# Sums, gates and weight preparations of a retention and two-FFN kernel, redistributed over the engines and stages of one core

## The chip, the core and the metric

The kernel runs on one core of one Trainium2 chip. TensorE (PE) multiplies matrices from SBUF into PSUM, VectorE (DVE), ScalarE (ACT) and GpSimd (POOL) work elementwise, and SyncE (SP) mostly issues DMA transfers; each engine executes its own instructions in the order in which they stand. The metric is the device time in microseconds of one launch. Before the change it is 1136.62 us, the median of 2 runs (1136.56 to 1136.67).

## The reference

A retention (linear attention with decay) feeds two feed-forward layers without residuals. Everything is float32; 3072 tokens, model width 512, inner width 2048:

```python
for t in range(S):                      # B, H, S, D = 4, 8, 768, 64
    state = gamma * state + k[:, :, t] (outer) v[:, :, t]
    y[:, :, t] = (1 / sqrt(D)) * q[:, :, t] @ state
x = y as (B * S, H * D)
h = x @ moe_w_in;   x = maximum(0.01 * h, h) @ moe_w_out          # leaky ReLU
h = x @ moe2_w_in;  x = (h / (1 + exp(-1.702 * h))) @ moe2_w_out  # gated by a sigmoid
```

The weights arrive as 64-bit floats, so the kernel itself turns each pair of 32-bit words into a float32.

## The kernel before

Every product is made of three matmuls on split operands: each float32 operand becomes a rounded high part (a cast on ACT) and a low part (a subtraction on DVE), and high*low, high*high and low*high are summed in PSUM. On top of that, each FFN product is done by a Strassen-Winograd scheme with 7 products instead of 8, whose operands and weights are sums and differences of quarter blocks. The program runs through six stages, and I give each a letter:

- **A, retention**, 24 steps, with the raw words of the first input weights loaded, converted and split beside it. The first tiles of FFN 1's input layer follow each step.
- **B**: 16 plain products `ffn_in(m, x1, ...)` of 12 matmuls with 256 columns, on the token columns left over. Each is emptied by ACT with a leaky ReLU, and stored with a DMA that ACT issues.
- **C, `First` of FFN 1** (`first1`): 24 pairs of (token block, q), 7 products of 6 matmuls with 384 columns each. `tick()` follows each product and runs whatever was put off by a number of ticks (`Later.at`), then `beside1`, which gives out at most one step of a weight preparation per tick.
- **D, `Second` of FFN 1** (`second1`): 168 items (3 blocks, 7 forms, 8 values of q), 6 matmuls of 512 columns per item. For each item ACT casts the operand (`high`, four items ahead), and DVE subtracts (`low`, three ahead); I call the latter a low. 96 operands' sums (`total`, four forms times 8 times 3) make the forms' operands from the loaded blocks; of these, the ones of form 5 are on DVE and the other 72 on POOL (`nc.gpsimd` given to `second1`).
- **E, `First` of FFN 2** (`first2`): 32 pairs, as C, with the sigmoid gate.
- **F, `Second` of FFN 2** (`second2`): as D, with all 96 sums on DVE, then a transpose and the store of the result.

A weight preparation (`Prep`) makes one half of a row of weights for a later stage: two loads of 256 KB of raw words, two ACT functions (`words_scalar`), four DVE operations (`words_vector`, lines 182 to 188), a rounding addition (`round_up`, line 197), three subtractions that form the Strassen sums (`total`, by way of line 157), and a store of 448 KB. There are 48, 16 each for `1o` (FFN 1 out), `2i` (FFN 2 in) and `2o`. Before, the first 20 (`N_P`) are done beside B and C, the next 15 (`N_S`) in D by the smaller form `Packed`, the last 13 in E; rounding and sums are on POOL in all three. SP's queue is in order too: a store of a sum that isn't there yet holds up the loads behind it.

The gate of E (`inner`, `gate`) is a Sigmoid on ACT into an extra tile, and a product on DVE with the value itself (line 615). The result then goes into `gd2` by a DMA that ACT issues.

Of the kernel before, what the change touches and what calls it, by code (L numbers as in the profile page):

```python
# [21 lines left out]
P = 128  # L22
# [10 lines left out]
T1 = 384  # L33
# [25 lines left out]
N_P, N_S = 20, 15  # L59
# [31 lines left out]
def retention_two_ffn(ctx: ExitStack, tc: tile.TileContext, qkv, consts, small, w1i, w1o, w2i, w2o, scratch, out):  # L91
# [167 lines left out]
    def retention():  # L259
# [129 lines left out]
        for s in range(len(steps)):  # L389
# [28 lines left out]
    class Prep:  # L418
# [36 lines left out]
        def steps(self):  # L455
# [4 lines left out]
            out = [lambda: None, lambda: words_scalar(self.f, self.low, raw[:, :, 1])]  # L460
            out += [lambda step=step: step(self.f, raw[:, :, 1]) for step in words_vector]
            return out

        def finish(self, clock, others, e=nc.gpsimd, wait=5):
            round_up(self.f, self.low, e)
            self.total(e)
            clock.at(wait, self.store)
            if others:
                others.pop(0).load()

    class Packed(Prep):
# [7 lines left out]
        def sums(self, e=nc.gpsimd):  # L479
# [48 lines left out]
    class First:  # L528


        def __init__(self, at, clock, src, dst, first, n, gated, weight, p_banks):
# [3 lines left out]
            self.g, self.s, self.p = (ring(at[k], T1) for k in ("g", "s", "p"))  # L535
# [37 lines left out]
        def run(self, done, step, beside):  # L573
# [19 lines left out]
            def inner(n, r, f, src=None, made=None):  # L593
# [15 lines left out]
                def gate(src, t):  # L609
                    s = next(self.s)[:, :w]  # L610
                    nc.scalar.activation(out=s, in_=src, func=AF.Sigmoid, scale=1.702)  # L611

                    def product():
                        dst = tile() if t is None else t
                        nc.vector.tensor_tensor(out=dst, in0=src, in1=s, op=ALU.mult)
                        later.at(2, lambda: store(dst))

                    later.at(1, product)

                if made is not None:  # L620
                    t = tile()
                    made(t)
                    if self.gated:
                        later.at(1, lambda: gate(t, t))
                        return
                    src, dst = t, t
                    later.at(1, lambda: nc.scalar.activation(out=dst, in_=src, func=AF.Lrelu))
                    later.at(3, lambda: store(dst))
                elif self.gated:
                    gate(src, None)  # L630
                else:
                    dst = tile()
                    nc.scalar.activation(out=dst, in_=src, func=AF.Lrelu)
                    later.at(2, lambda: store(dst))
# [596 lines left out]
```

## Time and profile before

| what | value |
|---|---|
| median of the runs | 1136.62 us |
| the profiled execution, its own time | 1130.26 us |
| its span, first to last instruction | 1128.5 us |
| PE busy | 1054.5 us, 93% of the span |
| DVE busy | 890.0 us, 79% |
| ACT busy | 616.8 us, 55% |
| POOL busy | 393.9 us, 35% |
| granted TensorE clock, mean | 0.978 |
| DMA | 241.63 MB, mean 214 GB/s |

How to read it: an engine's busy time covers the whole span, and a matmul's end is modelled, so a matmul that waits within its pipeline counts as busy. What bounds the kernel shows stage by stage, in the busy time of each engine within the stage, in the time that PE waits, and in the pace of PE. The granted clock is given in parts of full speed.

### The profile page before, as it was taken

What the parts mean: (1) busy time and instruction counts of PE and PEld (TensorE: products, weight loads), DVE (VectorE), ACT (ScalarE), POOL (GpSimd) and SP (SyncE); (2) the same over time, 40 slices, a digit from 0 to 9 for tenths busy, and PEclk for the clock granted to TensorE, in tenths of its full rate; (3) what the DMA queues carried; (4) which work ended last, traced back from release to release, by engine and by line L of the source; (5) the groups of instructions that cost most, each with busy time, mean ns of one, the idle gap of its engine ahead of it and who ended that gap; (6) DMA issues with size and microseconds to landing.
All of it is one profiled execution on the core that took longest, in us unless ns stands there. A gap on an engine that the chain in (4) does not pass through costs nothing.

```text
span 1128.5 us, 18170 instructions
## 1 busy us (share of the span) xinstructions
PE 1054.5 (93%) x6198; PEld 920.2 (82%) x6198; DVE 890.0 (79%) x1300; ACT 616.8 (55%) x1256; POOL 393.9 (35%) x353
## 2 busy tenths in 40 slices
PE   9999979999999869888888799999999999999998
PEld 6777878989998647656666499999999988888886
DVE  5998456886536999898889967768677899788786
ACT  5776355755666544443443476656566665544543
POOL 2332135675301684389349831343432000000000
PEclk9999989999999889998999999999999999999999
DMA  9999678889478454823744466564849852843723
GB/s 341 361 382 399 222 246 274 282 271 322 167 265 277 137 175 150 266 85 113 248 165 135 162 225 230 178 234 175 296 148 329 272 176 72 196 139 84 215 75 75
DMA packets 185420, 241.63 MB, mean 214 GB/s; under 512 B 59248, under 2 KB 134896, under 8 KB 182256
## 3 DMA queue, kind: packets, MB, share of 16 engines
q1 hardware_dynamic: 157376, 208.19, 55.5%
q10 hardware_dynamic: 27952, 32.29, 8.0%
q8 instruction: 48, 0.79, 0.3%
q14 instruction: 44, 0.36, 0.1%
HBM read 146.58 MB, written 93.85 MB: 213 GB/s over the span
## 4 chain that ended last, share of the span: by engine, by line
PE 56%; DVE 20%; DMA 11%; issue 5%; POOL 4%; ACT 2%; SPq 1%; ACTq 1%; DVEq 0%; POOLq 0%
PE psum L589 28%; PE psum L790 20%; DVE c L157 8%; PE psum L252 4%; DMA c<-w1o 2%; DVE h L157 2%; DMA h<-qkv 2%; POOL b L755 2%; DMA d<-gd 1%; DVE b L755 1%; DMA gd<-d 1%; PE psum L290 1%; DMA b<-gd 1%; PE psum L320 1%; DMA h<-wdt 1%
## 5 line engine op out<-in xcount | busy, mean ns | idle before, releaser
L790 PE MATMUL psum<-c,h 128*128 128x512 f32 x1008 | 258.6, 414 | 49.3 <-DVE c L157 45.9
L790 PEld LDWEIGHTS psum<-c,h 128*128 128x128 f32 x1008 | 195.7, 198 | 112.0 <-DVE c L157 66.8
L790 PE MATMUL psum<-e,h 128*128 128x512 f32 x768 | 179.3, 389 | 0.0
L790 PEld LDWEIGHTS psum<-e,h 128*128 128x128 f32 x768 | 144.1, 188 | 29.9
L742 ACT CAST c<-b 128x512 fp32r<-128x512 f32 x96 | 58.7, 621 | 97.9 <-PE psum L790 47.8
L589 PE MATMUL psum<-c,h 128*128 128x384 f32 x576 | 110.1, 334 | 0.3 <-DVE d L637 0.3
L589 PE MATMUL psum<-b,h 128*128 128x384 f32 x576 | 110.1, 334 | 0.2 <-ACT psum L673 0.2
L157 DVE TENSOR_TENSOR h<-h 128x256 fp32r<-128x256 f32 (+3 forms) x144 | 86.0, 636 | 30.1 <-ACT h L898 15.2
L157 DVE TENSOR_TENSOR c<-b,c 128x512 fp32r<-128x512 f32 x96 | 102.2, 1095 | 4.4 <-ACT c L742 3.8
L589 PEld LDWEIGHTS psum<-c,h 128*128 128x128 f32 x576 | 100.7, 188 | 0.6 <-DVE d L637 0.6
L589 PEld LDWEIGHTS psum<-b,h 128*128 128x128 f32 x576 | 100.7, 188 | 0.6 <-ACT psum L673 0.6
L611 ACT ACTIVATE d<-psum 128x384 f32<-128x384 f32 x96 | 47.1, 491 | 62.7 <-PE psum L589 56.2
L742 ACT CAST e<-a 128x512 fp32r<-128x512 f32 x77 | 47.7, 622 | 43.3 <-PE psum L790 21.9
L589 PE MATMUL psum<-f,h 128*128 128x384 f32 x336 | 67.5, 335 | 1.5 <-DVE b L637 1.5
L589 PE MATMUL psum<-d,h 128*128 128x384 f32 x288 | 59.2, 340 | 7.3 <-ACT psum L673 7.3
L755 POOL TENSOR_TENSOR d<-d,a 128x512 f32<-128x512 f32 x24 | 42.6, 1802 | 65.2 <-PE psum L790 65.2
L589 PEld LDWEIGHTS psum<-f,h 128*128 128x128 f32 x336 | 59.0, 188 | 2.0 <-DVE b L637 1.8
L637 DVE TENSOR_TENSOR psum<-psum,g 128x384 f32<-128x384 f32 x56 | 31.5, 563 | 36.6 <-PE psum L589 34.3
L157 DVE TENSOR_TENSOR e<-a,e 128x512 fp32r<-128x512 f32 x77 | 52.3, 685 | 8.3 <-ACT e L742 7.7
L589 PEld LDWEIGHTS psum<-d,h 128*128 128x128 f32 x288 | 51.1, 191 | 8.7 <-ACT psum L673 8.7
L589 PE MATMUL psum<-a,h 128*128 128x384 f32 x288 | 58.1, 337 | 0.1
L589 PE MATMUL psum<-e,h 128*128 128x384 f32 x288 | 57.5, 334 | 0.0
(186 smaller groups left out, 2064.1 us busy)
## 6 DMA issues: line engine op xcount, KB each, us to landing
gd<-d ACTq DMA_DIRECT2D x128, 192.0 KB, 3.8
h<-qkv SPq DMA_DIRECT2D x21, 1024.0 KB, 8.7
b<-gd SPq DMA_DIRECT2D x72, 256.0 KB, 4.5
d<-gd SPq DMA_DIRECT2D x72, 256.0 KB, 4.8
a<-gd SPq DMA_DIRECT2D x48, 256.0 KB, 5.2
c<-w1i SPq DMA_DIRECT2D x16, 512.0 KB, 7.7
c<-w1o SPq DMA_DIRECT2D x32, 256.0 KB, 4.8
e<-w2o SPq DMA_DIRECT2D x26, 256.0 KB, 4.2
```

The lines of the kernel that those rows point to most:

```text
L157: e.tensor_tensor(out=o, in0=x, in1=y, op=ALU.subtract)
L252: nc.tensor.matmul(out=h, lhsT=w[:, a, k], rhs=x[c][:, k], start=(i == 0), stop=(i == 3 * NP - 1), skip_group_check=True)
L290: nc.tensor.matmul(out=ps[:, e, n], lhsT=kT[r, n], rhs=qT[r, n], start=True, stop=True, skip_group_check=True)
L320: nc.tensor.matmul(out=out(n, e), lhsT=v[:, n, r], rhs=sm[:, e, n], start=(n < 2), stop=(c == 0), skip_group_check=True)
L589: nc.tensor.matmul(out=t, lhsT=w(k, a), rhs=x[:, b, k], start=(start and m == 0), stop=(m == 5), skip_group_check=True)
L611: nc.scalar.activation(out=s, in_=src, func=AF.Sigmoid, scale=1.702)
L637: nc.vector.tensor_tensor(out=o, in0=x, in1=y, op=ALU.add)
L742: nc.scalar.copy(out=t[:, 0], in_=self.block_of(*item))
L755: e.tensor_tensor(out=a(*s[0]), in0=a(*s[1]), in1=a(*s[2]), op=s[3])
L790: nc.tensor.matmul(out=t[:, j], lhsT=w[:, j, a], rhs=x[:, b], start=(new and q == 0 and m == 0), stop=(q == NQ - 1 and m == 2), skip_group ...
```

## The change

Six things change.

1. In D, the 72 operands' sums move from POOL to DVE (`total`); the argument that chose the engine is gone.
2. In all preparations, rounding and sums move from POOL to DVE. The six or seven steps of a preparation become four: the ACT pair, two DVE operations, two more, then rounding, sums, store (one tick later) and the next load.
3. The preparations are divided 26 / 6 / 16 over C, D and E, in place of 20 / 15 / 13. In D a `Packed` starts every 18 items from item 30, in place of every 9 from item 6.
4. E's gate is one ACT function, `Gelu_apprx_sigmoid`, straight into the tile that is stored. Sigmoid, product and the extra tiles fall away.
5. The raw words of the first three preparations are loaded in the last three steps of A, in place of the second tick of B.
6. Tiles and delays in C: the ring of six result tiles starts in another area, stores are issued 4 ticks after the ACT function instead of 2 (the last pairs: 2), preparations come every 4 or 5 ticks in B and 5 or 6 in C, and `second1` begins its loads one pair later, 2 ticks apart instead of 3.

The core of the diff:

```diff
-N_P, N_S = 20, 15
+N_P, N_S = 26, 6
...
+            if s >= len(steps) - 3:
+                todo[s - len(steps) + 3].load()
...
-            out = [lambda: None, lambda: words_scalar(self.f, self.low, raw[:, :, 1])]
-            out += [lambda step=step: step(self.f, raw[:, :, 1]) for step in words_vector]
-            return out
-
-        def finish(self, clock, others, e=nc.gpsimd, wait=5):
+            f, low, high, e = self.f, self.low, raw[:, :, 1], nc.vector
+            vector = lambda k: [step(f, high) for step in words_vector[k : k + 2]]
+            return [lambda: words_scalar(f, low, high), lambda: vector(0), lambda: vector(2), lambda: self.sums(e)]
+
+        def sums(self, e):
             round_up(self.f, self.low, e)
             self.total(e)
-            clock.at(wait, self.store)
-            if others:
-                others.pop(0).load()
+
+        def give(self, clock, behind, others):
+            def end():
+                clock.at(1, self.store)
+                if others:
+                    others.pop(0).load()
+
+            *steps, last = self.steps()
+            behind.extend(steps + [lambda: (last(), end())])
...
-        def sums(self, e=nc.gpsimd):
+        def sums(self, e=nc.vector):
...
-                def gate(src, t):
-                    s = next(self.s)[:, :w]
-                    nc.scalar.activation(out=s, in_=src, func=AF.Sigmoid, scale=1.702)
-
-                    def product():
-                        dst = tile() if t is None else t
-                        nc.vector.tensor_tensor(out=dst, in0=src, in1=s, op=ALU.mult)
-                        later.at(2, lambda: store(dst))
-
-                    later.at(1, product)
...
+                def gate(dst, src):
+                    if self.gated:
+                        nc.scalar.activation(out=dst, in_=src, func=AF.Gelu_apprx_sigmoid)
+                    else:
+                        nc.scalar.activation(out=dst, in_=src, func=AF.Lrelu)
+                    later.at(1 if self.gated else 4 if n + 2 < len(pairs) else 2, lambda: store(dst))
...
-                e = nc.vector if i == 5 else self.e
-                e.tensor_tensor(out=a(*s[0]), in0=a(*s[1]), in1=a(*s[2]), op=s[3])
+                nc.vector.tensor_tensor(out=a(*s[0]), in0=a(*s[1]), in1=a(*s[2]), op=s[3])
...
-    left = [5]
-
-    def beside1(free):
+    left, apart = [3], [4]
+
+    def beside(clock):
         left[0] -= 1
         if left[0] <= 0 and todo:
-            p = todo.pop(0)
-            left[0] = beside1.apart
-            behind.extend(p.steps()[1:] + [lambda: p.finish(later2, waiting, nc.gpsimd, 3)])
+            left[0] = apart[0] + len(todo) % 2
+            todo.pop(0).give(clock, behind, waiting)
...
-        if n >= 6 and n % 9 == 6 and packed:
+        if n >= 30 and (n - 30) % 18 == 0 and packed:
             packed.pop(0).start(later)
```

Three places of the program show how instructions move. The first is DVE in the first block of D. Here c is the ring of split operands (a low writes it), a, b and d are the loaded blocks, h the weights, e a result. Before:

```order
L157 TENSOR_TENSOR c_3324<-b,c_3324 128x512 x2
L157 TENSOR_TENSOR c_3324<-a,c_3324 128x512
L157 TENSOR_TENSOR c_3358<-a,c_3358 128x512 x2
L157 TENSOR_TENSOR c_3324<-a,c_3324 128x512 x2
L182 TENSOR_SCALAR f<-f 128x512
L184 TENSOR_SCALAR f<-f 128x512
L186 TENSOR_SCALAR f<-f 128x512
L188 SCALAR_TENSOR_TENSOR f<-f 128x512
L798 TENSOR_TENSOR e<-psum,e 128x1024
```

and now:

```order
L749 TENSOR_TENSOR d<-d,a 128x512
L157 TENSOR_TENSOR c_3466<-a,c_3466 128x512 x2
L749 TENSOR_TENSOR d<-d,a 128x512
L157 TENSOR_TENSOR c_3504<-a,c_3504 128x512
L749 TENSOR_TENSOR d<-d,a 128x512
L157 TENSOR_TENSOR h_418<-h_418 128x128 x2
L157 TENSOR_TENSOR c_3504<-a,c_3504 128x512
L157 TENSOR_TENSOR h_1548<-h_1548 128x128 x2
L157 TENSOR_TENSOR c_3466<-a,c_3466 128x512
L749 TENSOR_TENSOR d<-d,a 128x512
L157 TENSOR_TENSOR h_418<-h_418 128x128 x2
L792 TENSOR_TENSOR e<-psum,e 128x1024
```

The sums (line 749, before 755) now stand between the lows, and the four word operations of a preparation (lines 182 to 188) have left this stretch.

The second place is DVE in the early pairs of C: c and e are tiles of a preparation, h the factors' splits, and line 637 (now 632) is the addition in PSUM that a later product waits for. Before:

```order
L637 TENSOR_TENSOR psum<-psum,g 128x384
L182 TENSOR_SCALAR c_233<-c_233 128x512
L184 TENSOR_SCALAR c_1633<-c_1633 128x512
L186 TENSOR_SCALAR c_1633<-c_1633 128x512
L637 TENSOR_TENSOR a_490<-psum,g 128x384
L157 TENSOR_TENSOR h_418<-h_418 128x256
L157 TENSOR_TENSOR h_1542<-h_1542 128x512
L157 TENSOR_TENSOR h_418<-h_418 128x256
L188 SCALAR_TENSOR_TENSOR c_1633<-c_1633,c_233 128x512
```

and now:

```order
L182 TENSOR_SCALAR c_233<-c_233 128x512
L184 TENSOR_SCALAR e_80<-e_80 128x512
L186 TENSOR_SCALAR e_80<-e_80 128x512
L188 SCALAR_TENSOR_TENSOR e_80<-e_80,c_233 128x512
L197 ISA e_80<-c_233,e_80 128x1024
L157 TENSOR_TENSOR e_80<-e_80 128x256
L157 TENSOR_TENSOR e_80<-e_80 128x128 x2
L632 TENSOR_TENSOR b<-psum,g 128x384
```

Rounding (line 197) and the three subtractions of a preparation have come into DVE's queue, ahead of the addition that PE needs.

The third place is SP's queue at the end of A. xd takes the retention's results, the load of b brings C's first input back, the loads of h from wdt are the factors of C's weights, and the loads of c from w1o are raw words. Before:

```order
L215 DMA wdt<-e_80 128x1024
L167 DMA xd_3_68<-a 128x2x384
L169 DMA xd_3_68<-a 64x2x384 x2
L552 DMA b<-xd_1_66 128x3072
L894 DMA h_1542<-wdt 128x512
L894 DMA h_1542<-wdt 128x256
L894 DMA h_418<-wdt 128x256
L437 DMA c_233<-w1o 128x2x256 x6
```

and now:

```order
L215 DMA wdt<-e_80 128x1024
L439 DMA c_233<-w1o 128x2x256 x4
L167 DMA xd_3_68<-a 128x2x384
L169 DMA xd_3_68<-a 64x2x384 x2
L439 DMA c_233<-w1o 128x2x256 x2
L560 DMA b<-xd_1_66 128x3072
L894 DMA h_1548<-wdt 128x512
L894 DMA h_1548<-wdt 128x256
L894 DMA h_418<-wdt 128x256
```

Four of the six raw loads now stand ahead of A's last store, and two between it and the load of b.

## Rows read from the trace of the kernel before

**Rows 1.** Windows by stage, B to F: us, busy by engine, clock, DMA share, GB/s.
```profile
133.00:164.00 31.00, 25.65 (x209) 25.27 (x205) 12.55 (x16) 12.90 (x27) 9.45 (x7) 0.89 0.78 243
164.00:352.00 188.00, 178.70 (x1012) 176.17 (x1010) 119.26 (x179) 115.57 (x239) 82.89 (x86) 0.99 0.77 261
352.00:661.00 309.00, 260.13 (x1019) 197.68 (x1020) 279.96 (x307) 146.16 (x272) 197.94 (x149) 0.94 0.50 168
661.00:894.00 233.00, 232.47 (x1340) 231.83 (x1339) 173.03 (x313) 142.93 (x289) 67.70 (x69) 1.00 0.67 235
894.00:1128.50 234.50, 230.51 (x1020) 190.28 (x1018) 197.11 (x311) 116.85 (x200) 0.02 (x1) 1.00 0.51 137
```

**Rows 2.** Waits of PE over the span: us in total, times, longest.
```profile
PE psum L790 <- DVE c L157: 45.9, 24, 4.3
PE psum L589 <- ACT psum L673: 7.5, 5, 2.8
PE psum L252 <- ACT a L256: 5.4, 1, 5.4
```

**Rows 3.** Groups of DVE in D, two of its three lows: busy, mean ns.
```profile
L157 DVE TENSOR_TENSOR c<-b,c 128x512 fp32r<-128x512 f32 x92 | 99.5, 1113 | 4.4 <-ACT c L742 3.8
...
L157 DVE TENSOR_TENSOR c<-a,c 128x512 fp32r<-128x512 f32 x24 | 27.1, 1171 | 0.0
```

**Rows 4.** Groups of POOL in D, one of its three sums.
```profile
L755 POOL TENSOR_TENSOR d<-d,a 128x512 f32<-128x512 f32 x24 | 42.6, 1802 | 65.2 <-PE psum L790 65.2
```

**Rows 5.** Groups of DVE in F, where POOL is silent.
```profile
L755 DVE TENSOR_TENSOR a<-b,a 128x512 f32<-128x512 f32 x47 | 32.2, 685 | 5.3 <-DMA b<-gd 5.3
...
L798 DVE TENSOR_TENSOR c<-psum,c 128x1024 f32<-128x1024 f32 x9 | 11.0, 1217 | 0.0
```

**Rows 6.** Timeline of DVE early in D: start, us, what.
```profile
361.50 0.69 DVE L755 TENSOR_TENSOR b<-d,b 128x512 f32<-128x512 f32 x1
362.10 0.69 DVE L157 TENSOR_TENSOR c<-b,c 128x512 fp32r<-128x512 f32 x1
...
366.18 1.53 DVE L157 TENSOR_TENSOR h<-h 128x128 fp32r<-128x128 f32 x2
...
369.25 0.42 DVE L182 TENSOR_SCALAR f<-f 128x512 uint32<-128x512 uint32 x1
...
371.10 0.69 DVE L157 TENSOR_TENSOR c<-b,c 128x512 fp32r<-128x512 f32 x1
```

**Rows 7.** Timeline of POOL, the same place.
```profile
362.57 4.79 POOL L755 TENSOR_TENSOR d<-d,a 128x512 f32<-128x512 f32 x1 [65.21 <-PE psum L790]
```

**Rows 8.** Pace of PE: timeline in C, then a window within F.
```profile
339.84 1.20 PE L589 MATMUL psum<-f,h 128*128 128x384 f32 x6
340.88 1.20 PE L589 MATMUL psum<-a,h 128*128 128x384 f32 x6
...
931.00:959.00 28.00, 28.00 (x125) 23.20 (x124) 27.31 (x45) 15.17 (x28) 0.00 (x0) 1.00 0.26 72
```

**Rows 9.** Timeline of ACT in B, around the wait of PE.
```profile
149.01 1.23 ACT L898 CAST h<-h 128x256 fp32r<-128x256 f32 x3 [7.72 <-DMA h<-wdt]
...
151.85 0.67 ACT L178 ACTIVATE c<-c 128x512 f32<-128x512 f32 x1 [0.88 <-DMA c<-w1o]
```

**Rows 10.** Window at the end of A; timeline of SP's queue.
```profile
125.00:130.00 5.00, 5.00 (x73) 3.96 (x72) 2.25 (x3) 0.60 (x1) 0.00 (x0) 1.00 0.14 54
...
139.40 2.12 SPq L894 DMA_DIRECT2D h<-wdt  x3
```

**Rows 11.** Groups of ACT in E: the Sigmoid, the table load.
```profile
L611 ACT ACTIVATE d<-psum 128x384 f32<-128x384 f32 x96 | 47.1, 491 | 62.7 <-PE psum L589 56.2 <-DVE d L615 3.1 <-DVE d L637 1.7
...
L1032 ACT ACT_TABLE_LOAD x1 | 1.3, 1283 | 0.0
```

**Rows 12.** Groups of DVE in A: the rounding addition, where DVE does it.
```profile
L197 DVE CUSTOM_DVE_ANT_0 b<-c,b 128x1024 uint16<-128x1024 uint16 x9 | 6.1, 681 | 0.0
```

**Rows 13.** Waits of ACT, 125 to 350 us: one of several for C's result tiles.
```profile
ACT a L633 <- DMA gd<-a: 6.1, 3, 4.7
```

More of the change, by code (lines that the diff above doesn't have):

```diff
@@ L872, in rows @@
             return slice(n * T2, (n + 1) * T2)
+    c1 = Area("c1")
+    prep_rings = ring([(c2, 4), (c2, 8), (c2, 0)], 4, P, 2), ring(run_of(c1, 2, 4) + [(e4, 0)], 8, P)
+    names = [(kind, n) for kind in ("1o", "2i", "2o") for n in range(2 * NQ)]
+    todo = [Prep(*name, prep_rings) for name in names[:N_P]]
+    waiting, behind = todo[3:], collections.deque()
     retention()
@@ L953, in retention_two_ffn @@
         later2.tick()
[L954 removed]
+        beside(later2)
     def step1(n):
[L957 removed]
         if n == 0:
+            apart[0] = 5
             form(7, 0, 0, 1)
@@ L964, in step1 @@
             later2.at(9, factors[n + 3].low)
-        if n == 2 * NQ:
+        if n == 17:
             first1.g = ring(g_at[1], T1)
-        if n == 18:
-            assert not todo and not behind
-            second1.begin(later2, 0, NQ, 4, 24, 3)
+        if n == 19:
+            assert not todo
+            second1.begin(later2, 0, NQ, 4, 24, 2)
     def done_p(blk, q):
@@ L981, in done_p @@
             second1.loads(3 if q == NQ - 2 else 5)
-    first1.run(done_p, step1, beside1)
+    first1.run(done_p, step1, lambda free: beside(later2))
     while behind:
@@ L1031, in done1 @@
         if m == 51:
-            nc.scalar.activation(out=p_a.view(0, 4), in_=first2.raw[:, 0, :4], func=AF.Sigmoid, scale=1.702)
+            nc.scalar.activation(out=p_a.view(0, 4), in_=first2.raw[:, 0, :4], func=AF.Gelu_apprx_sigmoid)
         if m in (45, 47, 49):
@@ L1058, in retention_two_ffn @@
     todo = [Prep(*name, prep_rings2) for name in names[N_P + N_S :]]
-    behind, waiting = collections.deque(), []
+    behind, waiting, apart[0] = collections.deque(), [], 100
+    left[0] = 100
     def step2(n):
@@ L1067, in step2 @@
             todo[n - 4].load()
-        if n == 5:
+        if n == 6:
             waiting.extend(todo[2:])
-        if 6 <= n < 24 and n % NQ in range(1, 7) and todo:
-            p = todo.pop(0)
-            behind.extend([lambda: behind.extendleft(reversed(p.steps() + [lambda: p.finish(later2, waiting)]))])
+            left[0], apart[0] = 0, 7
         if n == 26:
@@ L1085, in done2 @@
         second2.loads(3 if q == NQ - 2 else 5)
-    def beside2(free):
-        if behind and free:
-            behind.popleft()()
-    first2.run(done2, step2, beside2)
+    first2.run(done2, step2, lambda free: beside(later2) if free or todo else None)
     while behind:
```

40 lines of the change are left out of this document (12 added, 28 removed).

## The prediction

> **What bounds the kernel now.** I read the windows by stage first, since one average over six stages with different limits says little. Then I read the waits of PE, the groups of DVE and POOL in the stage that loses most, and the timeline there, because means of contended work hide what an operation costs alone.
>
> The pace that PE can hold is the yardstick. In C a product of 6 matmuls starts 1.04 us after the one before; in F 125 matmuls of 512 columns fill 28 us, 0.224 us each [rows 8]. At that pace C needs 24 x 7 x 1.04 = 174.7 us and takes 188. D needs 168 x 6 x 0.224 = 225.8 us and takes **309**. E needs 32 x 7 x 1.04 = 233 us and takes 233, and F does the same matmuls as D in 234.5 with its tail [rows 1]. So E and F run at PE's pace, C loses 13 us, and D loses 83, more than all other stages.
>
> D's loss is DVE's lateness. [...] DVE is busy 280 of 309 us [rows 1], but a low in D takes 1113 to 1171 ns [rows 3], where the same shape takes 685 in F, with POOL silent [rows 5]. At 361.5 us, ahead of POOL's first sum, two such operations start 0.60 us apart [rows 6]. POOL's sum, begun at 362.57, lasts 4.79 us, while DVE goes on at its pace [rows 7], and then a pair of small DVE operations takes 1.53 us [rows 6]. So the two engines exclude each other where both read two SBUF operands: POOL's sums take 1.8 us on average [rows 4], and its 198 us in D [rows 1] are mostly paid for by DVE.
>
> **The change, part by part.**
>
> *D, sums and lows.* DVE gets the 72 sums (24 it has). There are 164 lows left in this stage and 96 sums, 260 operations. What does one cost when POOL is silent? Its duration is 0.69 us, but the next starts after 0.60 [rows 6], so I take 0.60: 156 us. To these come 11 evacuations of 1.2 us [rows 5], 13 us; 40 weight splits of 128 or 256 columns, some 12 us (pro rata from 0.60 for 512, an estimate); and 5 us of the next stage's forms. Preparations: six in place of 15. Four word operations take 371.10 - 369.25 = 1.85 us [rows 6], rounding 0.68 [rows 12], the three subtractions no more than 3 x 0.60, by their columns about 1.0. That is 3.5 us each, 21 for six. Sum: **207 us of DVE for 226 us of PE.**
>
> So PE becomes the bound of D. Locally it is closer: by the order, 38 of the 168 items have about 53 us of DVE work ahead of them (all the splits, a preparation, three forms' sums), and PE reaches that place after 51 us, with lows three items (4 us) ahead. Later blocks have less. I take 3 us of waiting: D falls from 309 to 229, **-80**. What is late next there would be ACT's casts, but ACT is busy 146 us now [rows 1] and loses nine preparations.
>
> [...] That such operations overlap is what the two starts in [rows 6] show, so the trace decides for 0.60; the durations remain as the dear end: 260 x 0.69 + 13 + 12 + 5 + 6 x 4.2 = 235 us, with 12.5 of lag at the worst place. D is then 243, -66. The cheap end is no wait at all, -83.
>
> *C, six more preparations, rounding and sums on DVE.* DVE receives 26 x (0.68 + 1.0) + 6 x 1.85 = 55 us. Its present 132 us in B and C [rows 1] shrink, as POOL keeps only the forms' sums there: with 0.09 us of overlap on some 200 operations and the contention gone, to 95 or 100. That makes 150 to 187 us of 219. As the preparations end by pair 18, the stretch in which they run is over nine tenths full, and the additions that PE waits for stand behind bursts of 1.3 us; PE goes on for three products, 3.1 us, before it needs one. I cost this at 3 us. Against that stand the 13 us that C loses now, of which 7.5 are waits for ACT's copies [rows 2], late behind raw words, forms and result tiles that land late [rows 13]. The loads now go out as soon as DVE has rounded, not after POOL's turn. The copies at C's start stay late, since B's ACT work grows by a preparation. I take half the loss as recovered, **-6**, from -13 (all) to +10 (DVE's durations, DMA as below).
>
> *First raw words in A.* B's wait of 5.4 us ends behind ACT [rows 2], and ACT's queue stood first 7.72 us for the factors from `wdt`, then 0.88 for raw words [rows 9]. The change takes away the latter, and puts the words' two functions (0.67 each) ahead of the wait: 2 us. The former stays. SP issues those loads at 139.4 [rows 10], and one of the three raw loads, 512 KB, now stands just before; at the 300 GB/s or so that such stretches move, it delays them by 1.7 us. The other two fall into a stretch with a DMA share of 0.14 [rows 10] and cost nothing. **-1**, between 0 and -7.
>
> *E, the gate.* DVE loses 128 products, and gets three more preparations and all sums. It was busy 173 of 233 us, and PE waits for neither engine there, so this gains nothing. ACT has the same 128 functions of 384 columns. The trace holds no Gelu; Sigmoid takes 491 ns [rows 11], and its cost lies between that and 0.67 us, the longest ACT function of [rows 9] (for 512 columns). ACT is busy 143 us of 233 [rows 1]: 128 x 0.18 more lies in that cover. Were the cover gone, it would cost 23 us. **0**, at most +6 where a block begins.
>
> *F and A*: nothing in them changes but A's loads. 0.
>
> Sum: -80 - 6 - 1 = -87. The profiled execution of 1130.26 us lies 6.4 below the median of 1136.62; its own would become 1043, and with the same distance the median **1050 us**.
>
> **The rivals.**
>
> *DVE stays the bound in D* (operations cost their durations, or words arrive late and hold its queue). For it: 94% DVE load at those prices, and a late start's lag isn't made good. Against it: F runs the same lows and sums with 197 us of DVE busy and no PE wait. -66 - 1 - 3: about 1066. Chance 0.18.
>
> *C is starved.* Six more preparations move 6 x 0.96 MB through a stage at a DMA share of 0.77 [rows 1], and result tiles are stored two ticks later in a ring of six, so that ACT, which already waits on this ring [rows 13], waits more. If C loses 10 more instead of 6 less: 1066 again, or 1080 with the first rival. Chance 0.12.
>
> *DVE's 1.1 us in D isn't POOL's doing* but that of PSUM, DMA or clock in this stage. Then the sums come on top, at the same rate: 280 us - 9 x 2.2 (words) + 72 x 1.1 + 6 x 3 = 357 us, 48 more than 309: 1136.6 + 48 - 7 = **1178**, slower. It decides at (309 - 51) / 260 = 0.99 us per operation. For it: only the means in [rows 3]. Against it: within the same stage, 0.60 us as long as POOL is held off [rows 6]. Chance 0.03.
>
> *The gate reloads tables.* If Gelu and the copies beside it didn't share a set, ACT would load a table (1283 ns, [rows 11]) at each change, some six per pair: 32 x 6 x 1.28 = 246 us on top of 143, 156 over E's 233: 1050 + 156 = 1206. The order has two table loads in the whole program, as before. Chance 0.01. [...]
>
> **How the numbers follow.** The forecast has 0.62; its own range is 1035 to 1062. The other 0.04 are things I haven't seen, half of them above 1080. With both dear ends (D -66, C +5) the time is 1075, with both cheap ones 1136.6 - 83 - 13 - 7 = 1033. The range is 1033 to 1076. Two per cent, 23 us either way, is about what a measurement tells from no change. Only the 1178 and 1206 cases and half of the unseen ones come out above 1113: faster 0.94, same 0.02, slower 0.04.
>
> **What would show it right or wrong.** Right: D's window about 229 us long with clock near 1.00, lows and sums near 0.69 us long and 0.60 apart, POOL nearly idle there until D's end, DVE's work in D about 207 us by starts (some 235 by durations). The wait on lows at most 5 us. C at 182, still with a wait at its start; B's wait on ACT still there, shorter. Wrong: lows above 0.9 us without POOL; waits of PE on line 632 in C of more than 8 us in total; DMA waits of ACT on C's tiles above 25; a Gelu above 0.67 us.

## The result, and the profile after

The changed kernel takes **1082.18 us**, the median of 2 runs (1082.13 to 1082.23), against 1136.62: a ratio of 0.952, 95% interval 0.948 to 0.956. Four further runs of it (e13 below) have a median of 1084.1 us and a ratio of 0.955, interval 0.9525 to 0.9574. The sign and the place of the gain were as forecast. The size was not: 1050 us was forecast, and 1082 lies outside the range of 1033 to 1076.

The profiled execution's span is 1080.4 us, and its own time 1082.13. A stage lasts from its first matmul to that of the next stage, which I read off PE's timeline:

| us | A | B | C | D | E | F | span |
|---|---|---|---|---|---|---|---|
| before | 133.4 | 30.5 | 188.2 | 307.4 | 234.6 | 234.4 | 1128.5 |
| after | 135.7 | 29.9 | 202.2 | 239.0 | 239.1 | 234.5 | 1080.4 |
| difference | +2.3 | -0.6 | **+14.0** | **-68.4** | +4.5 | +0.1 | -48.1 |
| forecast | 0 | -1 | -6 | -80 | 0 | 0 | -87 |

The windows of the changed kernel by stage, B to F, answer to [rows 1] (us, then busy by engine PE, PEld, DVE, ACT, POOL, clock, DMA share, GB/s):

```profile
136.00:166.00 30.00, 26.20 (x195) 26.00 (x194) 15.87 (x27) 14.35 (x30) 5.56 (x3) 0.89 0.74 241
166.00:368.00 202.00, 183.87 (x1011) 179.64 (x1010) 149.77 (x296) 118.67 (x248) 17.58 (x9) 0.97 0.78 269
368.00:607.00 239.00, 232.49 (x1012) 190.17 (x1012) 217.54 (x367) 136.65 (x252) 18.50 (x13) 0.99 0.53 179
607.00:846.00 239.00, 234.82 (x1348) 233.14 (x1347) 151.76 (x264) 147.45 (x296) 28.60 (x21) 1.00 0.70 243
846.00:1080.00 234.00, 230.34 (x1019) 189.94 (x1017) 195.31 (x307) 116.81 (x200) 0.00 (x0) 1.00 0.50 136
```

D (third row) has its clock back, 0.99 where [rows 1] showed 0.94, and POOL is down from 198 us to 18.5. DVE does more there in less time: 307 busy pieces took 280 us, now 367 take 217.5. C (second row) is longer and its clock lower, 0.97 for 0.99, though no engine is busy for more than 91% of it.

PE's waits over the whole span, after, answer to [rows 2] (line waited at, releaser: us in total, times, longest):

```profile
PE psum L597 <- ACT psum L668: 11.5, 5, 4.5
PE psum L784 <- DVE c L157: 6.5, 4, 3.9
...
PE psum L252 <- ACT b L256: 3.8, 1, 3.8
```

The wait for D's lows fell from 45.9 to 6.5 us. The wait for ACT's copies rose from 7.5 to 11.5, and its longest piece from 2.8 to 4.5; C has 7.3 us of the first sum and 10.9 of the second. PE's waits for DVE in C grew more: before they were one,

```profile
PE psum L589 <- DVE b L637: 1.5, 1, 1.5
```

and after they come to 6.4 us in six, with this as the largest part:

```profile
PE psum L597 <- DVE a L632: 2.6, 2, 1.4
```

The groups of DVE in D, after, answer to [rows 3, 5] (busy us, mean ns of one, idle before):

```profile
L157 DVE TENSOR_TENSOR c<-b,c 128x512 fp32r<-128x512 f32 x92 | 64.1, 709 | 8.3 <-ACT c L737 7.1
...
L749 DVE TENSOR_TENSOR d<-d,a 128x512 f32<-128x512 f32 x24 | 16.4, 682 | 0.0
L157 DVE TENSOR_TENSOR c<-a,c 128x512 fp32r<-128x512 f32 x24 | 15.9, 683 | 0.7 <-ACT c L737 0.7
```

A low takes 683 to 709 ns, not 1113 to 1171, and a sum on DVE 682 ns, not 1802 on POOL [rows 4]. DVE's timeline in D's first block, after, answers to [rows 6]:

```profile
397.31 0.68 DVE L157 TENSOR_TENSOR c<-d,c 128x512 fp32r<-128x512 f32 x1
397.92 0.68 DVE L749 TENSOR_TENSOR d<-d,a 128x512 f32<-128x512 f32 x1
398.52 0.68 DVE L157 TENSOR_TENSOR c<-d,c 128x512 fp32r<-128x512 f32 x1
399.12 0.68 DVE L749 TENSOR_TENSOR b<-b,a 128x512 f32<-128x512 f32 x1
```

Lows and sums alternate and start 0.60 to 0.61 us apart, on which the forecast's price rested. Each lasts 0.68 us, which as the price of one in such a row would be too dear, as the starts show.

The first thing that went wrong in C shows where PE stands longest. Four views of the changed kernel, around 194 us. PE:

```profile
193.44 1.20 PE L597 MATMUL psum<-e,h 128*128 128x384 f32 x6
199.13 2.29 PE L597 MATMUL psum<-d,h 128*128 128x384 f32 x6 [4.48 <-ACT psum L668]
```

ACT, whose copy (L668) PE needs, stood before it at the result tile:

```profile
197.82 0.49 ACT L621 ACTIVATE a<-psum 128x384 f32<-128x384 f32 x1 [6.62 <-DMA gd<-a]
198.21 0.48 ACT L621 ACTIVATE d<-psum 128x384 f32<-128x384 f32 x1
198.58 0.50 ACT L668 COPY psum<-psum 128x384 f32<-128x384 f32 x1
```

SP's queue, where the store of that tile (a) was issued only at 188.68, behind the 1.5 MB load of C's next block (b):

```profile
187.58 0.32 SPq L560 DMA_DIRECT2D b<-xd  x1
188.07 0.32 SPq L610 DMA_DIRECT2D gd<-d  x1
188.68 0.32 SPq L610 DMA_DIRECT2D gd<-a  x1
```

And DVE, stopped by the same kind of wait:

```profile
199.66 0.56 DVE L632 TENSOR_TENSOR d<-psum,g 128x384 f32<-128x384 f32 x1 [4.61 <-DMA gd<-d]
```

Read upwards: the store lands 9 us after its issue, ACT and DVE wait for the ring of six, and PE waits for ACT. Over B and C, ACT waits for such stores 21.7 us; before it was 12.6, of which [rows 13] shows 6.1. After the wait six matmuls take 2.29 us where 1.20 is usual, and the window right behind it has a granted clock of 0.50, where that of C as a whole has 0.97:

```profile
199.00:203.00 4.00, 3.87 (x12) 3.88 (x13) 2.76 (x6) 3.54 (x9) 1.52 (x1) 0.50 0.82 280
```

So this wait of 4.48 us cost more than its length.

### The profile page after: what moved, and what is told of

It is laid out like the page before. It is cut to its first block, busy times and chain, and to the rows that moved or that the text cites. A ratio compares the mean times of both kernels' runs of the same rounds, so it can differ in the third digit from the quotient of the medians.

```text
span 1080.4 us, 17732 instructions
## 1 busy us (share of the span) xinstructions
PE 1036.7 (96%) x6198; PEld 919.5 (85%) x6198; DVE 839.0 (78%) x1436; ACT 616.5 (57%) x1256; POOL 106.0 (10%) x89
## 4 chain that ended last, share of the span: by engine, by line
PE 76%; DVE 11%; DMA 8%; ACT 3%; issue 2%; ACTq 1%; SPq 0%; DVEq 0%
PE psum L784 38%; PE psum L597 29%; PE psum L252 4%; DMA h<-qkv 2%; PE psum L290 2%; DMA gd<-a 2%; PE psum L320 2%; DVE c L157 1%; DVE e L157 1%; DMA a<-xd 1%; DMA gd<-d 1%; PE psum L313 1%; PE psum L326 1%; DMA h<-wdt 1%; DVE f L157 1%
## 5 line engine op out<-in xcount | busy, mean ns | idle before, releaser
L784 PE MATMUL psum<-c,h 128*128 128x512 f32 x1008 | 232.3, 392 | 7.1 <-DVE c L157 6.5
L784 PEld LDWEIGHTS psum<-c,h 128*128 128x128 f32 x1008 | 189.6, 189 | 49.6 <-DVE c L157 9.3
L784 PEld LDWEIGHTS psum<-e,h 128*128 128x128 f32 x768 | 144.1, 188 | 30.1 <-DVE e L157 0.2
L597 PEld LDWEIGHTS psum<-c,h 128*128 128x128 f32 x576 | 100.5, 188 | 4.9 <-DVE d L632 3.3
L157 DVE TENSOR_TENSOR h<-h 128x256 fp32r<-128x256 f32 (+3 forms) x144 | 65.8, 499 | 42.6 <-ACT h L523 31.7
L157 DVE TENSOR_TENSOR c<-b,c 128x512 fp32r<-128x512 f32 x96 | 66.8, 708 | 8.3 <-ACT c L737 7.1
L597 PE MATMUL psum<-d,h 128*128 128x384 f32 x288 | 60.3, 345 | 12.3 <-ACT psum L668 10.9
L597 PE MATMUL psum<-a,h 128*128 128x384 f32 x288 | 60.3, 346 | 1.2 <-DVE a L157 1.2
L597 PEld LDWEIGHTS psum<-a,h 128*128 128x128 f32 x288 | 53.1, 197 | 1.5 <-DVE a L157 1.5
L597 PEld LDWEIGHTS psum<-e,h 128*128 128x128 f32 x288 | 51.3, 191 | 1.6 <-DVE e L157 1.3
```

The lines of the kernel that those rows point to most:

```text
L157: e.tensor_tensor(out=o, in0=x, in1=y, op=ALU.subtract)
L597: nc.tensor.matmul(out=t, lhsT=w(k, a), rhs=x[:, b, k], start=(start and m == 0), stop=(m == 5), skip_group_check=True)
L784: nc.tensor.matmul(out=t[:, j], lhsT=w[:, j, a], rhs=x[:, b], start=(new and q == 0 and m == 0), stop=(q == NQ - 1 and m == 2), skip_group ...
```

## The experiments

All start from the changed kernel. The times are medians where there were several runs (e13, e14, e17: four each), else single runs. C of the six kernels in which nothing of C is changed (the changed kernel, e4, e7, e8, e11, e13) is 202.2, 206.6, 202.2, 204.7, 204.6 and 203.9 us: **204.0** on average, and a difference below some 3 us in C says nothing. D of the same kernel repeats within 1 us.

**e1: stores two ticks after the ACT function.**
```diff
-later.at(1 if self.gated else 4 if n + 2 < len(pairs) else 2, lambda: store(dst))
+later.at(1 if self.gated else 2, lambda: store(dst))
```


> The changed kernel with C's result tiles stored 2 ticks after the ACT function again, not 4; nothing else. Theory 1 (late stores: a ring of six tiles leaves 5 to 7 ticks between a store's issue and the tile's next use, and a store behind a 1.5 MB load takes 9 us): ACT's waits for gd stores in C fall from 21.7 us to about 10, and C (202 us in the changed kernel) shortens by 8 to 12 us, the whole to about 1072. Theory 2 (six more preparations fill DVE and DMA): C stays within 3 us of 202, the whole at 1080 to 1084.


1078.03 us; C 197.8, 6 less. ACT's wait for stores falls from 21.7 to 10.3 us:

```profile
ACT b L621 <- DMA gd<-b: 4.9, 2, 3.0
...
ACT a L621 <- DMA gd<-a: 4.0, 2, 3.1
...
ACT d L621 <- DMA gd<-d: 1.4, 2, 1.2
```

PE's wait for ACT's copies in C halves with it, from 10.9 to 5.4 us. One cause of C's loss, but less than half of it.

**e2: 20 preparations beside B and C, 12 in D.**
```diff
-N_P, N_S = 26, 6
+N_P, N_S = 20, 12
-        if n >= 30 and (n - 30) % 18 == 0 and packed:
+        if n >= 30 and (n - 30) % 9 == 0 and packed:
```


> The changed kernel with 20 preparations beside C and 12 in D (every 9 items from item 30), stores late as in the change. Theory 1 (late stores): C shortens by 4 us at most, still near 198 to 202, with ACT's waits for gd stores near 20 us. Theory 2 (six more preparations): C falls back to 188 to 192. In either case D gets 6 x 3.5 = 21 us more of DVE work: if DVE is close to its limit there, as 207 us of 229 by starts says, D grows by 5 to 15 us.


1094.40 us. C 199.5 (-4.5), but D 253.9 (+14.9), where PE's wait for lows is 14.8 us again. In C, PE's waits for DVE fall from 6.4 to 3.7 us, while ACT's wait for stores stays (23.1). A preparation costs more in D than in C.

**e6: both, e1 and e2.**


> The changed kernel with both edits of the first two runs: C's stores after 2 ticks, and 20 / 12 / 16 preparations. Each alone shortened C by 4.4 and 2.7 us. If late stores and a full DVE are separate causes, both together give 194 to 196 for C; if one hides the other, C falls under 192, near the 188 of the kernel before; if neither is the cause, 198 or more. D as with 20 / 12 / 16 alone, 254.


1085.97 us; C **191.2**, 12.8 less than 204.0, where the two alone made 6.2 and 4.5; D 253.6. The two causes add up to within the scatter of C. Together they are nearly the whole of C's loss: before had 188.2.

**e3: a preparation's next raw load three ticks later.**
```diff
-                    others.pop(0).load()
+                    clock.at(3, others.pop(0).load)
```


> The changed kernel with a preparation's next load issued 3 ticks after its sums, not in the same tick (in C and E). Theory 3 (SP stands before the load until DVE has rounded, 43 us in C, and holds the result tiles' stores behind it): SP's waits for rounding fall under 10 us, ACT's waits for gd stores fall by half or more, C shortens by 5 to 10 us. Theory 1 (the stores are late by their own ticks, and behind the 1.5 MB loads): C shortens by less than 3 us.


1081.87 us, C 204.9: no effect. But SP stands as long in e3, 61.3 us for preparations over C, against 63.1 in the changed kernel; it only does so before their stores in place of their loads. So this run doesn't test whether SP's standing delays the result tiles. e2 bears on that: SP stands there for 49.6 us, and ACT's wait for the stores is no shorter.

**e4: D's 72 sums back on POOL.**
```diff
-                nc.vector.tensor_tensor(out=a(*s[0]), in0=a(*s[1]), in1=a(*s[2]), op=s[3])
+                (nc.vector if i == 5 or self.src is not gd1 else nc.gpsimd).tensor_tensor(out=a(*s[0]), in0=a(*s[1]), in1=a(*s[2]), op=s[3])
```


> The changed kernel with the 72 operands' sums of D back on POOL; all else as changed. Theory of the prediction (DVE and POOL exclude each other where both read two SBUF operands): lows in D go back over 1.0 us, D grows from 240 to 285 or more, the whole to 1125 to 1140. Rival (D was freed by the nine preparations fewer, not by the sums): lows stay near 0.7 us and D under 250, the whole under 1092.


1127.43 us, D 281.9, a little under the 285 expected: **+42.9** by this alone. PE's wait for lows in e4:

```profile
PE psum L784 <- DVE c L157: 37.0, 20, 5.9
```

The groups of DVE and POOL in e4's D:

```profile
L157 DVE TENSOR_TENSOR c<-b,c 128x512 fp32r<-128x512 f32 x91 | 92.2, 1041 | 6.3 <-ACT c L737 5.8
L157 DVE TENSOR_TENSOR c<-d,c 128x512 fp32r<-128x512 f32 x48 | 33.6, 710 | 16.4 <-ACT c L737 16.3
...
L749 POOL TENSOR_TENSOR d<-d,a 128x512 f32<-128x512 f32 x24 | 41.3, 1747 | 131.0 <-PE psum L784 70.0 <-DMA a<-gd 57.3 <-DVE b L749 3.7
```

The lows on b are back at 1041 ns, those on d keep their 710 ns. So what lengthened those on b was neither PSUM, DMA nor the stage, but POOL's sums: they take 709 ns without these and 1041 with them. The rest of D's 68 us, 25, wasn't tried apart. Before, the lows on d were slow too:

```profile
L157 DVE TENSOR_TENSOR c<-d,c 128x512 fp32r<-128x512 f32 x48 | 53.4, 1160 | 0.4 <-ACT c L742 0.4
```

POOL then also did the preparations' rounding and sums, 61 us of its 198 in D, and in e4 it is busy for 133. So the same lengthening, beside POOL's work on the preparations, is a likely part of the 25 us, beside the nine preparations that D has fewer.

**e5: rounding and sums of the preparations in C and E on POOL**, stores two ticks later.
```diff
-            f, low, high, e = self.f, self.low, raw[:, :, 1], nc.vector
+            f, low, high, e = self.f, self.low, raw[:, :, 1], nc.gpsimd
-                clock.at(1, self.store)
+                clock.at(3, self.store)
```


> The changed kernel with the preparations' rounding and sums in C and E on POOL again, their store 3 ticks later as before; all else as changed. Theory 4 (C is late since DVE is full: its waits at the block boundaries near 240 and 305 us stand behind rounding and sums): the waits of PE on DVE in C (about 8 us) vanish, C falls from 202 to 195 or less, E from 239 to 236. Rival (POOL's sums block DVE's two-input operations as they did in D, so that freeing DVE of 1.7 us per preparation costs it as much in blocking): C and E stay within 2 us of 202 and 239 or grow.


1089.10 us; C 208.0 (+4.0), E 242.2 (+3.1). Both lie about 1 us above what the kernels that are the same in that stage reach (C 206.6, E 241.3), so that POOL is no better a place there, and moving them to DVE isn't what lengthened C or E. That DVE is the better one isn't shown by so little.

**e15 and e16: by what the six further preparations cost C.** Both with e1's stores; e15 leaves out their DVE work, e16 their loads.
```diff
+            if self.kind == "2i" and self.q * 2 + self.hh >= 4:          # e15, in steps()
+                return [lambda: words_scalar(f, low, high), lambda: None, lambda: None, lambda: None]
...
+            if self.kind == "2i" and type(self) is Prep and self.q * 2 + self.hh >= 4:   # e16, in load()
+                return
```


> Result tiles stored after 2 ticks, and the six further preparations of C leave out their word operations, rounding and sums on DVE (some 21 us of DVE); their ACT functions, loads and stores stay. If those six cost C by DVE's time in its queue: C 191 to 193 us, as with 20 preparations and this store (191.2). If they cost by DMA or by ACT: C stays near 197.8.

> Result tiles stored after 2 ticks, and the six further preparations of C leave out their loads of raw words (3 MB); ACT, DVE and stores stay. If those six cost C by DMA: C 191 to 194 us. If by DVE's time: C near 197.8, as with their loads.


Without the DVE work C is **192.5** us (1074.92 us in all), without the loads 198.0 (1078.80), against 197.8 with both. The window over C of e1:

```profile
165.00:362.00 197.00, 181.79 (x1011) 176.53 (x1009) 154.57 (x296) 119.45 (x249) 17.79 (x9) 0.98 0.81 274
```

The same of e15:

```profile
167.00:359.00 192.00, 179.95 (x1010) 175.73 (x1009) 133.67 (x251) 120.80 (x250) 17.56 (x9) 0.99 0.83 283
```

And of e16:

```profile
166.00:364.00 198.00, 180.81 (x1012) 176.10 (x1012) 155.69 (x300) 121.10 (x251) 17.83 (x9) 0.99 0.75 259
```

DVE loses 21 us of work in e15, and C 5. With a DMA share of 0.75 in place of 0.81, e16 gains nothing. So DVE at 154 of 197 us costs a quarter of what is added to it, and the six loads cost nothing here. The six stores were not left out by themselves; but e15, which keeps loads and stores, comes within 1.3 us of the 191.2 of e6, where the six are gone altogether. Nor does the gain come by way of SP's queue and the result tiles: PE's waits for DVE in C fall from 9.2 us (e1) to 5.4, while those for ACT's copies (5.4 and 5.9) and ACT's for stores (10.3 and 14.8) don't.

**e9 and e10: where a preparation's DVE work stands in C**, both with e1's stores. e9 gives no preparation a step in the last pair of a block, and starts them every 5 ticks in C in place of 5 or 6; e10 puts an empty step behind the ACT functions, so that DVE doesn't stand in wait for them.
```diff
-    first1.run(done_p, step1, lambda free: beside(later2))
+    first1.run(done_p, step1, lambda free: None if first1.last else beside(later2))      # e9
...
-            left[0] = apart[0] + len(todo) % 2
+            left[0] = apart[0] + (len(todo) % 2 if apart[0] != 5 else 0)      # e9
...
-            return [lambda: words_scalar(f, low, high), lambda: vector(0), lambda: vector(2), lambda: self.sums(e)]
+            return [lambda: words_scalar(f, low, high), lambda: None, lambda: vector(0), lambda: vector(2), lambda: self.sums(e)]   # e10
```


> The changed kernel with C's stores after 2 ticks, and no step of a preparation in the last pair before a block's end (preparations every 5 ticks elsewhere in C). Theory 4 (PE's waits on DVE at C's block ends, 6.5 us with stores after 2 ticks, come from rounding and sums that stand before the next block's forms): those waits fall under 3 us, C from 197.8 to 193 to 195. Rival (DVE is full in all of C, so that work moved from one place waits at another): C stays at 197 to 200.

> The changed kernel with C's stores after 2 ticks, and one empty step between a preparation's ACT pair and its first DVE pair (C and E). Theory 5 (E's 4.6 us come from DVE standing at the word operations until a late ACT has made the words, 15.5 us in 8 waits, with the additions that PE needs behind them): those waits fall under 6 us, E from 239.6 to 236 or less. Rival (E's waits come from rounding and sums, which are on DVE now): E stays at 239 to 240.


e9: 1076.88 us, C 200.2, no gain over e1's 197.8; ACT's wait for stores is 18.8 us again. e10: 1072.58 us, C 195.5; its three relatives below have 196.2, 197.2 and 196.8. The mean of the four is 196.4, 1.4 below e1's single run: too little to call shown. The expectation was on E. DVE's waits there for the words fall from 19.6 us (e1) to 4.6, and E still lasts 238.9 us, for 239.6 in e1, so those waits aren't what lengthened E.

**e11: the gate as before**, with three tiles for the Sigmoid and seven in place of ten for results.
```diff
-                        nc.scalar.activation(out=dst, in_=src, func=AF.Gelu_apprx_sigmoid)
+                        s = next(self.s)[:, :w]
+                        nc.scalar.activation(out=s, in_=src, func=AF.Sigmoid, scale=1.702)
+
+                        def product():
+                            nc.vector.tensor_tensor(out=dst, in0=src, in1=s, op=ALU.mult)
+                            later.at(2, lambda: store(dst))
+
+                        later.at(1, product)
+                        return
```


> The changed kernel with E's gate as before: Sigmoid on ACT into an extra tile, product on DVE, store 2 ticks after it. By the prediction the gate bought no time by itself, since PE was E's bound: E within 2 us of 239. Rival (the three preparations more and the sums fit into E only because the products left DVE): E grows by 5 us or more, to 244 and up, with waits of PE on DVE.


1095.65 us; E **253.9**, 14.8 more, nothing else changed beyond the scatter. E's window in e11, with DVE at 208 us for 152 now:

```profile
606.00:860.00 254.00, 240.13 (x1349) 236.10 (x1348) 207.77 (x390) 145.67 (x297) 28.23 (x21) 0.99 0.66 228
```

ACT's waits in e11's E, with new ones for DVE:

```profile
ACT d L621 <- PE psum L598: 39.6, 44, 1.7
ACT d L621 <- DVE d L624: 16.1, 10, 4.5
ACT d L621 <- DVE d L640: 14.7, 8, 3.3
```

ACT waits 16.1 us for the product (L624) to free a tile. How much of the 14.8 is DVE's load, and how much the smaller rings, this run doesn't separate.

**e12: first raw words loaded in B again**, the first preparation two ticks later.
```diff
-            if s >= len(steps) - 3:
-                todo[s - len(steps) + 3].load()
...
-    left, apart = [3], [4]
+    left, apart = [5], [4]
+    first3 = todo[:3]
-    early_steps = {1: lambda: factors[0].load(slice(2, 3)), 2: lambda: factors[1].load(),
+    early_steps = {1: lambda: (factors[0].load(slice(2, 3)), [p.load() for p in first3]), 2: lambda: factors[1].load(),
```


> The changed kernel with the first three preparations' raw words loaded in the second tick of B again, and the first preparation at the fifth tick, as before. By the prediction the early loads are worth 1 us (0 to 7): B 30 to 31 instead of 28 to 30, with PE's wait in B at 4 to 6 us. Rival (the preparation that comes earlier crowds ACT at C's start, where PE waits 3.6 us): B grows, but C shortens by as much or more.


1089.93 us; B 30.9, where all others have 27.7 to 29.9, and C 206.5, at the upper end of its scatter. The early loads, with the first preparation two ticks sooner, are worth 1 to 3 us in B.

**e7 and e8: two trials on D.** e7 puts the last splits of E's factors on DVE, e8 starts D's preparations at item 57.
```diff
-                later.at(3 + 2 * u, lambda u=u: w_split(u, 3, 7, nc.gpsimd))
+                later.at(3 + 2 * u, lambda u=u: w_split(u, 3, 7))                  # e7, and two like it
...
-        if n >= 30 and (n - 30) % 18 == 0 and packed:
+        if n >= 57 and (n - 57) % 18 == 0 and packed:                              # e8
```


> The changed kernel with the splits of FFN 2's first weights, at the end of D, on DVE in place of POOL. Theory (POOL's last work in D blocks DVE, whose operations there take 1.7 to 2.3 us in place of 0.7 to 1.2, and PE waits 3.9 us): that wait goes, D falls from 239 to 235 or less. Rival (DVE is short of time there anyway, and gets 18 subtractions, 7 us): the wait stays or grows, D at 239 to 244, or E begins late.

> The changed kernel with D's six preparations started at items 57, 75 ... 147, not 30, 48 ... 120. Theory (DVE's lag is worst in D's first block, where all the weight splits stand, and a preparation on top makes PE wait 2.1 us near 421): that wait goes, D shortens by 2 to 3 us. Rival: the later preparations meet the forms and splits at D's end, and D's last wait of 3.9 us grows by as much; D stays at 239 or more.


e7: 1083.75 us, D 238.6, nothing gained. Without splits on POOL, DVE's lows at D's end take 0.69 us and its early sums 0.95 and 0.96; but DVE has the splits to do as well, and PE's late waits, 4.4 us in the changed kernel, still come to 3.8, in four pieces. e8: 1086.83, D 243.1, worse by 4; its last preparation starts at item 147 of 168. Which of them costs it I didn't look into.

**e13 and e14: the changed kernel again, and a better one.** e14 is e10 with D's preparations from item 45, every 15.
```diff
-        if n >= 30 and (n - 30) % 18 == 0 and packed:
+        if n >= 45 and (n - 45) % 15 == 0 and packed:
```


> The changed kernel itself once more, beside the next three, for the size of what varies from run to run. If the differences of 4 to 6 us found in C so far are real: C again 202 to 206 us, the median 1081 to 1084, the others' C below by what was found for each. Rival (chance of placement or of DMA timing): C below 200 or above 208.

> Three steps together: C's result tiles stored after 2 ticks, an empty step between a preparation's ACT functions and its DVE operations, and the six preparations of D from item 45, every 15. If the first two make room for C by what they did before (C 195.5): C 194 to 197, and D 237 to 239, since no preparation falls into its first 45 items: 1068 to 1073. Rival: the starts from 45 crowd D's end, where POOL's splits stand, D 241 or more and no gain over 1072.6.


e13: 1084.1 us (1081.54 to 1086.43), C 203.9, D 239.6. e14: **1074.57 us** (1072.33 to 1076.23; 1068 to 1073 was expected), ratio to before 0.947, interval 0.945 to 0.949, which doesn't touch that of e13. C 196.2, D 237.5. It beats both kernels, the changed one by some 9.5 us.

**e17 and e18: what is left in D**, both from e14. e17 starts the first three splits on POOL four items later; e18 leaves out the DVE work of D's six preparations.
```diff
-                later.at(3 + 2 * u, lambda u=u: w_split(u, 3, 7, nc.gpsimd))
+                later.at(7 + 2 * u, lambda u=u: w_split(u, 3, 7, nc.gpsimd))       # e17
...
-            words(self.f, self.low, raw[:, :, 1])                                  # e18, and its rounding and sums
+            words_scalar(self.f, self.low, raw[:, :, 1])
```


> The kernel of e14, and the three splits of factors on POOL at D's end start four items later (from the tick of item 7 after form 6, not 3). In e14 POOL's 11.25 us of splits meet DVE's early sums and lows (2.04, 1.90, 1.78 us each), and PE then waits 3.91 us. If that meeting makes the wait: it falls below 1.5 us, D 233 to 236 against 237.5, the median some 2 to 4 us below 1074.6, unless E's start waits for the splits in its turn. Rival (the forms and early sums on DVE are too much by themselves, or the meeting only moves): the wait stays near 4 us or stands at E's start, D plus E unchanged at 476.

> The kernel of e14, and the six preparations of D leave out their word operations on DVE, rounding and sums (some 21 us of DVE); ACT, loads and stores stay. If DVE has room for them in D, as forecast: D 236 to 238, as in e14 (237.5). Rival (DVE is still the bound in D, by so much as it has more to do): D falls by 5 us or more, to 232.


e17: 1074.56 us, D 237.7, not the 233 to 236 expected. The wait at D's end isn't gone, it came later. PE in e17:

```profile
594.08 5.99 PE L784 MATMUL psum<-c,h 128*128 128x512 f32 x18 [3.40 <-DVE c L157]
```

POOL in e17, with the splits before it:

```profile
581.24 13.37 POOL L157 TENSOR_TENSOR h<-h 128x512 fp32r<-128x512 f32 x8 [277.15 <-ACT h L160]
```

e18: 1074.94 us, D 236.4, 1.1 us less, hardly more than D's scatter, for 16.5 us less of DVE's busy time (217.0 in e14's D, 200.4 here). PE in e18's D:

```profile
396.01 182.40 PE L779 MATMUL psum<-c,h 128*128 128x512 f32 x804
578.88 1.65 PE L779 MATMUL psum<-c,h 128*128 128x512 f32 x6 [0.47 <-DVE c L157]
584.45 14.92 PE L779 MATMUL psum<-c,h 128*128 128x512 f32 x54 [3.92 <-DVE c L157]
```

804 matmuls without a wait, 182.40 / 804 = 0.2269 us each: PE's own pace, and only then waits of 0.47 and 3.92 us. DVE has room for six preparations in D if they stand 15 items apart away from its ends.

## Why the prediction was wrong, point by point

**The step that failed is C, "-6".** It was +14, and with it went 20 of the 38.9 us by which the spans missed. The rival "C is starved" had priced 10 more for it and 0.12 of chance. Its two parts were both there: stores two ticks later in a ring of six (e1: some 6 us), and six more preparations (e2, e15: some 5). But the second works by DVE's time and not by the transfers that the rival named first (e15, e16). The sum put the late stores at nothing, as they were named in the rival only, and DVE's bursts at 3 us because PE "goes on for three products". That cover didn't hold: PE's waits for DVE in C rose from 1.5 to 6.4 us, and the wait of 4.48 us for ACT came by ring and queue, which a count of products leaves out. The half of C's old loss that was to come back didn't: the waits for ACT's copies, from which it was to come, grew from 7.3 to 10.9 us. The signs set for C were too coarse to tell: PE's waits on line 632 there came to 3.0 us (8 was the sign) and ACT's for stores to 21.7 (25). And the range took C at +5 at most, where the part on C allowed +10.

Some 3 us of C's +14 (191.2 in e6 against 188.2) stay unexplained. That lies at the scatter of C, and 188.2 comes from one execution, of 1130.26 us, where the other 19 of the same kernel took 1132.69 to 1138.17.

**D, "-80", was right in its cause and too large by 11.6 us.** e4 settles the cause: with the 72 sums on POOL D is 42.9 us longer. The forecast's condition of two SBUF operands was too narrow: in D before, the word operation of line 182, which reads one, took 1.51 to 1.53 us beside POOL's work and 0.41 to 0.43 without, while the addition with one operand in PSUM (line 798) took 1.21 to 1.22 either way. The rival that the 1.1 us wasn't POOL's doing is refuted. "DVE stays the bound" isn't what happened either: D's price of 0.60 us held, e18 finds 1.1 us in 16.5 us of DVE's time, and PE ran 714 matmuls in a row without a wait:

```profile
423.97 162.73 PE L784 MATMUL psum<-c,h 128*128 128x512 f32 x714 [1.24 <-DVE c L157]
```

So it is by luck that the 1080 which the forecast gave for both rivals together lies next to the 1082 measured. DVE's work in D was 217.5 us where 207 had been counted. The term was mis-sized in several small places. I read the stage as its window of 309 us, and it lasted 307.4: 1.6. The pace of 0.224 us came from a count in a window that also holds the matmuls cut by its edges; at the 0.2269 of e18's long stretch D needs 228.7 us: 2.9. Of lateness 3 us were allowed. The first block lost 2.7 (236 matmuls in 56.2 us), and D's end 4.4 of waits and 1.7 by the lower clock behind them (0.76 over 7 us): 5.8 too much. That makes 10.3 of the 11.6. At the end DVE's operations are long beside POOL's again, in a new place. PE in the changed kernel, and the window behind its wait:

```profile
592.73 14.16 PE L784 MATMUL psum<-c,h 128*128 128x512 f32 x54 [3.92 <-DVE c L157]
...
593.00:600.00 7.00, 7.00 (x25) 5.38 (x25) 7.00 (x9) 4.27 (x8) 1.06 (x2) 0.76 0.09 25
```

DVE ahead of it:

```profile
585.33 1.78 DVE L157 TENSOR_TENSOR c<-b,c 128x512 fp32r<-128x512 f32 x1
587.03 2.05 DVE L565 TENSOR_TENSOR a<-a 128x768 f32<-128x768 f32 x1
589.11 1.90 DVE L566 TENSOR_TENSOR a<-a 128x768 f32<-128x768 f32 x1
590.94 1.74 DVE L157 TENSOR_TENSOR c<-b,c 128x512 fp32r<-128x512 f32 x1
```

And POOL beside it:

```profile
582.56 11.27 POOL L157 TENSOR_TENSOR h<-h 128x512 fp32r<-128x512 f32 x6 [274.48 <-ACT h L160]
```

A low takes 1.78 us beside POOL's splits. In e17, with the splits later, the same early sums take 0.95 and 0.96 us, and the lows behind them are the late ones; in e7, without splits on POOL, no low there takes more than 0.70 us. The forecast counted "POOL nearly idle there until D's end" and put no price on the end. This is as in e4, where a low took 1041 ns beside POOL's sums and 709 without: 1.78 us here beside the splits, for the 0.69 of the lows without POOL.

**E, "0", was +4.5, and the reason given did not hold.** The forecast took the gate as free of gain because PE waited for neither engine. But it added three preparations and all their sums to DVE in the same sentence, and the gate is what made room for them: undone, with the smaller rings that it needs, E is 14.8 us longer (e11). PE's waits in E are now 4.2 us, 3.6 of them for DVE's addition (line 632), where they were 0.5. What puts DVE behind there stays open: neither its rounding and sums (e5) nor its waits for words (e10) account for it, and 13 preparations in place of 16 weren't tried. The Gelu's own price was right. The group of ACT in E, after, answers to [rows 11]:

```profile
L619 ACT ACTIVATE d<-psum 128x384 f32<-128x384 f32 x95 | 46.5, 493 | 59.3 <-PE psum L597 57.5 <-ACT d L619 1.0
```

493 ns, against 491 for the Sigmoid.

**B, "-1", was -0.6, by the reason given.** ACT in B, after, answers to [rows 9]:

```profile
151.85 1.23 ACT L898 CAST h<-h 128x256 fp32r<-128x256 f32 x3 [8.28 <-DMA h<-wdt]
```

The wait for the factors stayed (8.28 us for 7.72), the one for raw words went, and PE's wait fell from 5.4 to 3.8. **F**, 0, held to 0.1 us. **A**'s +2.3 isn't shown to be an effect of the change: over the eighteen runs A lies between 133.6 and 138.3 us, just above the one 133.4 of before, and e12, which takes the early loads out of A, has 136.4.

**The offset.** The sum was made against a profiled execution 6.4 us below its median, and the same distance was added at the end. The changed kernel's profiled execution lies 0.05 us below its median. By spans the forecast missed by 38.9 us (C 20, D 11.6, E 4.5, A 2.3, the rest 0.5), and the vanished offset gave 6.4 of it back.

## What to carry to other kernels

When one engine's work slows another's, as POOL's sums did DVE's lows (1041 ns for 709), moving it can pay even onto the engine that looks full: DVE took over 72 sums, and its busy time in that stage fell from 249.6 us (e4) to 217.5. A term that is dismissed because the engines have time left must be checked against the rings and queues of that stage: a store two ticks later behind a 1.5 MB load cost 6 us, with PE, ACT and DVE all under 92% busy. And an edit that frees an engine should be costed together with the edit that fills it, since the second's price is what the first is worth.

## What the runs showed that I had not expected

- Preparations have no fixed price. Six more of them cost 5 us in C and 15 us in D, where twelve then stand 9 items apart (e2); the DVE work of six in all, 15 items apart, costs 1.1 us there (e18).
- A wait saved at D's end isn't saved: with POOL's splits later (e17) or on DVE (e7), D stays within 0.5 us of what it was. As I read it, the work there is too much for its place, whoever does it.
- Most of what one execution differs from the next by lies in A, where PE waits for `qkv` loads (3.0 to 6.1 us in total), and in C: 4.7 and 4.4 us between kernels that are the same in these stages, while F differs by 0.4.
